# A hand-planned attention and gated-MLP kernel: the planner's rule for the shared SBUF port, and two kinds of work that may move from GpSimd to VectorE

## The chip, the cores and the metric

The kernel runs on one core of a Trainium2 chip. A core has five engines that run their own instruction streams: TensorE (PE in the profile; its weight loads are PEld), VectorE (DVE), ScalarE (ACT), GpSimd (POOL) and SyncE (SP), which only issues DMAs. They work on SBUF, the on-chip memory, and on PSUM, where TensorE leaves its sums. The metric is the device time of one execution in microseconds (us); less is better.

## The reference

There are eight batches of 576 positions with eight heads of 64. Each head's attention is the sum of two: one over q, k and v averaged in groups of four positions (144 of them), repeated fourfold, and one over the band of positions closer than four.

```python
q_d, k_d, v_d = (mean over groups of 4 positions)
out_up = np.repeat(sm_attn(q_d, k_d, v_d), 4, axis=2)
scores = np.where(abs(i - j) < 4, scale * q @ k.T, -1e9)
out_local = softmax(scores) @ v
x = (out_up + out_local), heads side by side: (8, 576, 512)

h = np.maximum(x @ w_in, 0)                 # 512 -> 1024
u, v = h[..., :512], h[..., 512:]
v_n = (v - mean(v)) / sqrt(var(v) + 1e-6)
v_s = w_spatial @ v_n + b_spatial           # over the 576 positions
out = (u * v_s) @ w_out
```

## The kernel before, in words

Two heads are worked on together, on 64 partitions each, so there are 32 **attentions**, n = 0 to 31, four to a batch. An attention has, in the kernel's own names: a load of q and k (`qk`) and of windows of v (`v`); `sum1` and `sum2`, which add q and k in groups of four (lines 523 and 526, on GpSimd) and `sum3`, which scales and spreads q's sums; `S`, the band's scores on TensorE (line 553), then `mask`, `max`, `sub`, `exp`, `sum`, `inv` and `norm`, a softmax; `T`, its transposes (line 606); `AV` (line 686), the product with v; and for the averaged part `Sd` (line 618), `maxd`, `expd`, `invd`, `normd`, `Td` (654) and `AVd` (672). `xf` adds both parts, and `xhi` and `xlo` (lines 703 and 705) split the sum in two numbers of TensorE's 32-bit format, since every large product is made of three such partial products. `load_down` brings the averaged v: one DMA by SyncE's queue (`tv0`, line 494) and three that add onto it in memory, by GpSimd's queue (`tv`, line 496); each of the four waits until the one before has landed.

A batch's gated MLP then has five blocks `V` (line 732; the fifth, of 64 positions, is line 737) for the half that is normalized, eight `U` (786), eight `SP` over the positions (lines 804 to 807), and five `O` (834, 839). A `V` block is followed by relu, statistics on VectorE, `rstd` on GpSimd (759), `apply` on VectorE (746), `vhi` on ScalarE (763) and `vlo` (765). These share four row buffers, and four PSUM banks (`pm`).

The weights of w_in and w_out come as 64-bit floating point. Twelve pieces (`piece64`) take them apart on VectorE with integer operations (`e1`, `m1`, `m2`, `e3`), on ScalarE (`e2`), multiply mantissa and power of two on GpSimd (`m3`, line 424), and split the result (`whi`, `wlo`). w_spatial comes as 32-bit and is only split. All weights are decoded while the first attentions run.

**The order** is not the program's. Every operation is handed to a `Plan` with its engine, a duration in ns, its buffers, whether it uses the SBUF port that VectorE and GpSimd share (`port=True`), and a rank. `Plan.run` then goes through a simulated time: for every engine it takes, of the operations that could start within `NEAR` ns of the first that could, the one of the lowest rank; among the engines' candidates it emits the earliest. That fixes the order of the instructions on each engine, which then run in that order and wait for one another by semaphores. The ranks of an attention's steps are its number n plus the entries of `RANK` (one for batch 0, one for batch 1, one for all later ones), and those of a batch's blocks come from `MRANK`. `ON` says, by a letter for each attention or block, which of several engines does an operation (a `Way`): D is VectorE, P is GpSimd, A is ScalarE; the last letter holds for all that follow. For `mask`, T lets TensorE add the mask by two more matmuls (line 546), so that VectorE doesn't add it. Before 110 us of planned time, planned idle of TensorE is filled with matmuls on constants (`warm`, line 872).

Of the kernel before, what the change touches and what calls it, by code (L numbers as in the profile page):

```python
# [15 lines left out]
ALU = mybir.AluOpType  # L16
# [60 lines left out]
class Plan:  # L77
# [54 lines left out]
    def run(self, near=150.0, stay=0.0, dma=(1500.0, 4.2, 500.0), emit=True):  # L132
# [3 lines left out]
        port = 0.0  # L136
# [4 lines left out]
        mode = "F"  # L141
# [7 lines left out]
        while left:  # L149
            best = None  # L150
            for eng, ops in todo.items():
                t0 = free[eng]
                first, found = None, []
                for o in ops:
                    t = o.ready if o.ready > t0 else t0
                    if o.port and port > t:
                        t = port
                    if o.mode:
                        t += TURN[mode + o.mode]
# [24 lines left out]
            t, o = best  # L184
# [52 lines left out]
RANK = {"load": [17.851, 23.264, -5.516],  # L237
        "tv": [12.974, 22.991, -23.395],
        "sum": [2.845, 5.024, -10.777],
        "S": [10.209, 18.391, 8.905],  # L240
        "E": [7.352, 3.618, -15.279],
        "N": [4.14, 4.621, -14.612],
        "T": [-15.681, 6.591, 2.05],
        "Sd": [-48.304, -1.568, 6.234],
        "Nd": [3.291, -4.748, 39.225],
        "Td": [-6.413, -29.413, 1.538],
        "AVd": [5.75, -12.653, -2.551],
        "AV": [-15.213, 2.555, -20.265],
        "X": [-1.494, 10.399, 1.329]}
MRANK = {"V": [[-0.574, 0.623], [2.224, 0.01], [-11.217, 0.975]],  # L250
        "U0": [[2.087, 0.31], [1.571, 0.675], [1.966, 0.126]],
        "S0": [[-14.652, 7.66], [4.784, 0.04], [8.452, 0.274]],
        "U1": [[5.341, 132112000.0], [-12.254, 4.82], [3.082, 3.0]],
        "O0": [[25.153, 0.02], [8.915, 8.0], [13.043, 2.786]],
        "S1": [[-8.328, 0.085], [-22.165, 0.04], [2.505, 0.191]],
        "O1": [[-2.911, 13597.0], [9.3, 0.531], [7.824, 0.451]]}
EVICT = 8.0
WRANK = {"WV": [2.481, 0.044],
        "WU": [3.142, 1.539],
        "WSP": [-1.507, 1.688],  # L260
        "WO": [-21.154, 0.035]}
NEAR = 109.733
STAY = 18.724
# [4 lines left out]
ON = {"mask": "TTDDD",  # L268
# [7 lines left out]
def tile_kernel(ctx, tc, qk, vw, v4, w_in, wT, bsp, w_out, out, emit=True):  # L276
    nc = tc.nc
# [640 lines left out]
```

## Time and profile before

| | |
|---|---|
| median of 3 runs | 639.61 us (637.89, 639.61, 641.01) |
| the profiled execution's own time | 635.72 us |
| its span, from the first to the last record | 633.8 us |
| mean granted clock of TensorE | 0.976 of full speed |
| busy: TensorE, VectorE, ScalarE, GpSimd | 592.8, 412.1, 307.3, 229.7 us |
| moved by DMA | 56.95 MB |

The profile is of one execution, whose time of 635.72 us is 1.9 us more than its span and lies 3.9 us under the median of the runs. A busy time of TensorE holds also the filling matmuls of the start. A wait is put down to the instruction that ended last before it, and the chain of waits goes back from the last instruction to what released each one. Section 2 of the page cuts the span in 40 slices of 15.8 us.

### The profile page before, as it was taken

The page shows a single profiled execution, that of the slowest core. Times are in us where ns is not written, and L with a number is a line of the kernel's source. Part 1 is how long each engine was busy: PE and PEld are TensorE (multiplying, and loading weights), DVE is VectorE, ACT ScalarE, POOL GpSimd, SP SyncE. Part 2 cuts the span into 40 slices and gives each one's busy share as a digit, 9 for nine tenths or more (in the row PEclk, how much of TensorE's full clock was granted, in tenths as well). Part 3 has the DMA queues.
Part 4 walks back from the last instruction along what each step waited for, and adds up shares of the span by engine and source line. Part 5 has one row for each costly group of instructions (what it writes and reads, how often), then busy time and mean ns, then how long its engine had stood idle before and what let it go on. Part 6 is the DMA issues. An engine that isn't in the chain of part 4 may idle for free.

```text
span 633.8 us, 14573 instructions
## 1 busy us (share of the span) xinstructions
PE 592.8 (94%) x5987; PEld 518.9 (82%) x5987; DVE 412.1 (65%) x887; ACT 307.3 (48%) x790; POOL 229.7 (36%) x220
## 2 busy tenths in 40 slices
PE   5737998999999999998999979999899999999997
PEld 2415777988998889887898878988798888998895
DVE  5898989989769566585647565485756756334230
ACT  3537766564544455544554354443655455424222
POOL 6574464514324352145413462044521452004100
PEclk9778898999999999999999979999999999999999
DMA  9982643544017123243404323054222201000102
GB/s 241 281 200 82 187 99 110 148 103 133 23 57 199 25 60 100 83 107 55 134 9 156 58 72 100 2 169 57 77 84 90 61 24 42 1 35 1 51 1 74
DMA packets 37382, 56.95 MB, mean 90 GB/s; under 512 B 3650, under 2 KB 24130, under 8 KB 37316
## 3 DMA queue, kind: packets, MB, share of 16 engines
q1 hardware_dynamic: 35012, 48.94, 25.4%
q0 software_dynamic: 2304, 7.08, 7.2%
q8 instruction: 47, 0.77, 0.5%
q14 instruction: 19, 0.16, 0.1%
HBM read 46.57 MB, written 9.44 MB: 88 GB/s over the span
## 4 chain that ended last, share of the span: by engine, by line
PE 75%; DVE 11%; POOL 4%; issue 4%; DMA 3%; ACT 3%; POOLq 0%; ACTq 0%; DVEq 0%
PE pmb L834 5%; PE pma L804 5%; PE pmc L786 5%; PE pma L834 5%; PE pmd L786 5%; PE pmb L804 4%; PE pmc L804 3%; PE pmd L804 3%; PE pma L786 3%; PE pmb L786 2%; PE pmd L834 2%; PE pmc L732 2%; PE pmc L834 2%; PE paa L686 2%; PE pma L732 2%
## 5 line engine op out<-in xcount | busy, mean ns | idle before, releaser
L804 PE MATMUL pma<-wsp,vha 128*128 128x320 f32 (+1 forms) x240 | 36.8, 302 | 0.0
L705 POOL TENSOR_TENSOR xa<-xfa,xa 128x576 fp32r<-128x576 f32 x6 | 11.2, 1865 | 70.3 <-ACT xa L703 70.3
L804 PEld LDWEIGHTS pma<-wsp,vha 128*128 128x128 f32 x240 | 33.6, 188 | 0.0
L834 PE MATMUL pmb<-wo,ga 128*128 128x512 f32 x132 | 33.0, 399 | 0.0
L804 PE MATMUL pmb<-wsp,vha 128*128 128x256 f32 (+1 forms) x192 | 30.2, 308 | 0.0
L834 PEld LDWEIGHTS pmb<-wo,ga 128*128 128x128 f32 x132 | 24.2, 188 | 5.1
L804 PEld LDWEIGHTS pmb<-wsp,vha 128*128 128x128 f32 x192 | 27.5, 196 | 0.9 <-issue 0.8
L526 POOL TENSOR_TENSOR kdb<-suma 128x288 f32<-128x288 f32 x16 | 14.5, 905 | 36.5 <-PE pmb L618 33.9
L834 PE MATMUL pma<-wo,ga 128*128 128x512 f32 x108 | 27.3, 402 | 0.0
L523 POOL TENSOR_TENSOR suma<-qka 128x576 f32<-128x576 f32 x17 | 20.9, 1231 | 17.1 <-DMA qka<-qk_dram 16.8
L804 PE MATMUL pmd<-wsp,vha 128*128 128x256 f32 (+1 forms) x168 | 25.1, 298 | 0.0
L523 POOL TENSOR_TENSOR suma<-qkb 128x576 f32<-128x576 f32 x15 | 18.0, 1203 | 17.8 <-DMA qkb<-qk_dram 17.2
L804 PE MATMUL pmc<-wsp,vha 128*128 128x256 f32 (+1 forms) x168 | 24.2, 293 | 0.0
L834 PEld LDWEIGHTS pma<-wo,ga 128*128 128x128 f32 x108 | 19.7, 188 | 5.2 <-issue 1.0
L804 PEld LDWEIGHTS pmd<-wsp,vha 128*128 128x128 f32 x168 | 23.1, 188 | 0.2 <-issue 0.2
L804 PEld LDWEIGHTS pmc<-wsp,vha 128*128 128x128 f32 x168 | 22.7, 188 | 0.1
L566 DVE TENSOR_TENSOR sa<-pab,mask 128x384 f32<-128x384 f32 (+1 forms) x28 | 12.4, 482 | 15.7 <-PE pab L553 15.7
L872 PE MATMUL pma<-mask_b,mask_a 128*128 128x512 bf16 x62 | 18.4, 437 | 3.2 <-DVE mask_a L325 3.2
L594 ACT ACTIVATE sa<-sa 128x640 f32<-128x640 f32 x17 | 12.5, 738 | 18.3 <-DVE sa L572 18.2
L496 POOL DMA_DIRECT2D tva<-v_dram x12 | 10.9, 909 | 23.5 <-DMA tva<-v_dram 23.1
L496 POOL DMA_DIRECT2D tvb<-v_dram x12 | 10.4, 866 | 24.4 <-DMA tvb<-v_dram 24.0
L705 POOL TENSOR_TENSOR xb<-xfa,xb 128x576 fp32r<-128x576 f32 x7 | 10.2, 1450 | 24.7 <-ACT xb L703 24.7
(568 smaller groups left out, 1838.8 us busy)
## 6 DMA issues: line engine op xcount, KB each, us to landing
qka<-qk_dram SPq DMA_DIRECT2D x17, 576.0 KB, 4.0
qkb<-qk_dram SPq DMA_DIRECT2D x15, 576.0 KB, 5.7
stg<-w_in_dram SPq DMA_DIRECT2D x8, 512.0 KB, 5.3
tva<-v_dram POOLq DMA_DIRECT2D x12, 288.0 KB, 5.7
tvb<-v_dram POOLq DMA_DIRECT2D x12, 288.0 KB, 4.5
out_dram<-rowc SPq DMA_DIRECT2D x9, 256.0 KB, 2.3
va<-vw_dram SPq DMA_DIRECT2D x11, 192.0 KB, 4.4
vb<-vw_dram SPq DMA_DIRECT2D x11, 192.0 KB, 3.2
```

The source lines that it names most:

```text
L496: plan.op("POOL", 850, lambda r=r: nc.gpsimd.dma_start(t.ap, v4[b, r], accum_op=ALU.add), w=[t], rank=rank + 2.0 + 0.3 * r, kb=288, name="tv")
L523: nc.gpsimd.tensor_tensor(sb.ap.rearrange("p x (g r) -> p x g r", r=2), x[:, :, :, :2], x[:, :, :, 2:], op=ALU.add)
L526: nc.gpsimd.tensor_tensor(kb.ap, sb.ap[:, :, ::2], sb.ap[:, :, 1::2], op=ALU.add)
L566: nc.vector.tensor_tensor(sv, pv, mask[:, None, None, :].broadcast_to(list(pv.shape)), op=ALU.add)
L594: plan.op("ACT", 643, lambda: nc.scalar.activation(s.ap, s.ap, AF.Exp, scale=1.0 / 8.0), w=[s], rank=R["E"], name="exp")
L686: nc.tensor.matmul(pv.ap[h * 64:h * 64 + 64, c:c + QB[w + 1] - QB[w]], vb.ap[k, w], pT.ap[k, blk, q0:q0 + QB[w + 1] - QB[w]], start=True, ...
L705: plan.op(xl, 0, lambda: side(xl).tensor_sub(x.ap[:, 1, :], xf.ap, f(x.ap[:, 0, :])), r=[xf, x.sub(0)], w=[x.sub(1)], rank=R["X"], name="xlo")
L732: nc.tensor.matmul(ps.ap, xs[c].ap[:, i, t * P:(t + 1) * P], win[:, c, j, FF:], start=(c == 0 and (i, j) == (0, 0)), stop=(c == NC - 1 and ...
L786: nc.tensor.matmul(ps.ap[:, :n], win[:, c, i, ft * P:(ft + 1) * P], xs[c].ap[:, j, HA[h]:HA[h + 1]], start=(c == 0 and (i, j) == (0, 0)), ...
L804: nc.tensor.matmul(ps.ap[:, :n], vh.ap[:, c, i, fs], wsp[:, c, j, hs], start=(c == 0 and (i, j) == (0, 0)), stop=False)
L834: nc.tensor.matmul(ps.ap, g.ap[:, c, o1:o1 + P], wo[:, c, j, :], start=(c == 0 and (i, j) == (0, 0)), stop=(c == NF - 1 and i == 1))
L872: nc.tensor.matmul(ap.rearrange("p (j k) -> p j k", k=64), mask_a, mask_b[:, None, :].broadcast_to([P, 8, 64]), start=True, stop=True)
```

## The change

Three things change. In `Plan.run` the engines' candidates are now compared by the time at which they ask to start: when their inputs, buffers and engine are free. Before, they were compared by the time at which they could start, with the wait for the port and TensorE's change of tile shape in it. So the port goes to the one that asks first. `sum1` and `sum2` of an attention, and `m3` of a weight piece, become a `Way` and may run on VectorE. And all tables of ranks and of engines are new numbers, which reorders the program on every engine.

```diff
@@ Plan.run
-                    if o.port and port > t:
-                        t = port
-                    if o.mode:
-                        t += TURN[mode + o.mode]
 ...
                     if ok:
-                        found.append((t, o.rank - stay if o.mode == mode else o.rank, o))
+                        ask = t
+                        if o.port and port > t:
+                            t = port
+                        if o.mode:
+                            t += TURN[mode + o.mode]
+                        found.append((t, o.rank - stay if o.mode == mode else o.rank, ask, o))
 ...
-                t, _, o = min((x for x in found if x[0] <= first + near), key=lambda x: (x[1], x[0]))
-                if best is None or t < best[0]:
-                    best = (t, o)
+                t, _, ask, o = min((x for x in found if x[0] <= first + near), key=lambda x: (x[1], x[0]))
+                if best is None or ask < best[0]:
+                    best = (ask, t, o)
 ...
-RANK = {"load": [17.851, 23.264, -5.516],
-        "tv": [12.974, 22.991, -23.395],
+RANK = {"load": [-6.425, 5.791, -0.091],
+        "tv": [-13.62, 1.562, -8.346],
 ...
-ON = {"mask": "TTDDD",
-        "norm": "PDDDDDPDD",
-        "xlo": "DDDDDPDPP",
-        "normd": "ADDAPAAAD",
-        "vlo": "DPPDPDDDDPP"}
+ON = {"sum": "DDPPDDDPD",
+        "m3": "DDPPPPDDDDDD",
+        "mask": "TTTTTTTTD",
+        "norm": "PDDDDPDDD",
+        "xlo": "PDPDPDDPP",
+        "normd": "APAAAAADP",
+        "vlo": "PDPPPPPPPPP"}
 ...
         def m3():
-            nc.gpsimd.tensor_tensor(mb.ap, mb.ap, eb.ap, op=ALU.mult)
+            if pr.eng == "POOL":
+                nc.gpsimd.tensor_tensor(mb.ap, mb.ap, eb.ap, op=ALU.mult)
+            else:
+                nc.vector.scalar_tensor_tensor(mb.ap, mb.ap, 2.0**-20, eb.ap, op0=ALU.mult, op1=ALU.mult)
 ...
-        plan.op("POOL", 1251, m3, r=[eb], w=[mb], rank=rank, port=True, name="m3")
-        return split(dst_hi, dst_lo, lambda: mb.ap, 2.0**-20, [mb], rank, FF, key)
+        pr = Way("m3", {"WV": 0, "WU": NC, "WO": 2 * NC}[key[0]] + key[1], P=("POOL", 1251, True), D=("DVE", 602, True))
+        plan.op(pr, 0, m3, r=[eb], w=[mb], rank=rank, name="m3")
+        return split(dst_hi, dst_lo, lambda: mb.ap, 2.0**-20 if pr.eng == "POOL" else 1.0, [mb], rank, FF, key)
 ...
-        plan.op("POOL", 1150, sum1, r=[qkb], w=[sb], rank=R["sum"], port=True, name="sum1")
-        plan.op("POOL", 660, sum2, r=[sb], w=[kb], rank=R["sum"], port=True, name="sum2")
+        s1 = Way("sum", n, P=("POOL", 1150, True), D=("DVE", 669, True))
+        s2 = Way("sum", n, P=("POOL", 665, True), D=("DVE", 370, True))
+        plan.op(s1, 0, sum1, r=[qkb], w=[sb], rank=R["sum"], name="sum1")
+        plan.op(s2, 0, sum2, r=[sb], w=[kb], rank=R["sum"], name="sum2")
```

By the tables, VectorE takes over 29 of the 32 pairs of sums and 8 of the 12 `m3`; GpSimd takes `normd` of all attentions from 8 on (VectorE had them) and every `vlo` but one; TensorE adds the mask for 8 attentions (before 2). In numbers of instructions VectorE has 58 sums, 8 `m3`, 12 mask additions fewer (two for each of 6 attentions), 25 `normd` fewer and 5 `vlo` fewer. The changed kernel's lines lie 4 to 10 below those of before: line 523 becomes 531, 705 becomes 715, 496 becomes 504.

Three places show what moved. The first is VectorE ahead of the first `V` block, where the fourth attention's `xd` (its `xlo`, the last input of that block) is made. Before it is VectorE's 114th instruction, and the masks and maxima of attentions 4 and 5 and a piece of w_spatial stand ahead of it:

```order
L598 TENSOR_TENSOR sa<-sa,sma 128x640
L566 TENSOR_TENSOR sb<-paa,mask 128x2x3x64
L566 TENSOR_TENSOR sb<-paa,mask 128x2x2x64
L696 TENSOR_TENSOR xfa<-pab,dnb 128x2x116 x2
L698 TENSOR_TENSOR xfa<-pab,dnb 128x112
L569 TENSOR_REDUCE mxb<-sb 128x10
L378 SCALAR_TENSOR_TENSOR wsp<-stg,wsp 128x576
L631 TENSOR_SCALAR smdb<-smdb 96x3
L632 RECIPROCAL smdb<-smdb 96x3
L572 TENSOR_TENSOR sb<-sb,mxb 128x640
L705 TENSOR_TENSOR xd<-xfa,xd 128x576
```

Now it is the 100th, and among what stands ahead is an `m3` (line 431):

```order
L594 TENSOR_REDUCE sma<-sa 128x10
L382 SCALAR_TENSOR_TENSOR win<-rowd,win 128x512
L416 SCALAR_TENSOR_TENSOR rowa<-stg,rowa 128x512
L706 TENSOR_TENSOR xfa<-paa,dnb 128x2x116 x2
L708 TENSOR_TENSOR xfa<-paa,dnb 128x112
L431 SCALAR_TENSOR_TENSOR rowb<-rowb,rowa 128x512
L406 TENSOR_SCALAR rowc<-stg 128x512
L715 TENSOR_TENSOR xd<-xfa,xd 128x576
```

The second is GpSimd where a batch's `V` blocks begin, in batches 3 to 5 (numbered from 0). Before, the three adding DMAs of `tv` stand after both of the batch's last `xlo`, the third of them behind the first `rstd` (line 759) and ahead of the first `vlo` (765):

```order
L705 TENSOR_TENSOR xb<-xfa,xb 128x576
L523 TENSOR_TENSOR suma<-qka 128x576
L496 DMA tva<-v_dram 72x1024
L526 TENSOR_TENSOR kdb<-suma 128x288
L496 DMA tva<-v_dram 72x1024
L759 TENSOR_TENSOR stc<-stc,mhalf 128x1
L496 DMA tva<-v_dram 72x1024
L765 TENSOR_TENSOR vha<-rowb,vha 128x512
L759 TENSOR_TENSOR sta<-sta,mhalf 128x1
```

Now the first of them stands ahead of the last `xlo`, and the other two follow each other ahead of the first `rstd`:

```order
L715 TENSOR_TENSOR xa<-xfa,xa 128x576
L504 DMA tva<-v_dram 72x1024
L651 TENSOR_TENSOR eda<-eda,smda 96x432
L715 TENSOR_TENSOR xb<-xfa,xb 128x576
L504 DMA tva<-v_dram 72x1024 x2
L769 TENSOR_TENSOR stc<-stc,mhalf 128x1
L775 TENSOR_TENSOR vha<-rowc,vha 128x512
L769 TENSOR_TENSOR sta<-sta,mhalf 128x1
```

The third is VectorE at the end of such a batch, where a `sum1` now stands in its queue (line 531; it reads the q and k of the attention after next, whose load can start when the scores of the attention just masked are done), ahead of the next `maxd` and `xf`:

```order
L576 TENSOR_TENSOR sb<-pab,mask 128x2x3x64
L576 TENSOR_TENSOR sb<-pab,mask 128x2x2x64
L579 TENSOR_REDUCE mxb<-sb 128x10
L582 TENSOR_TENSOR sb<-sb,mxb 128x640
L594 TENSOR_REDUCE smb<-sb 128x10
L531 TENSOR_TENSOR suma<-qkb 128x576
L632 TENSOR_REDUCE mxda<-pma 96x3
L706 TENSOR_TENSOR xfa<-paa,dnb 128x2x116 x2
L708 TENSOR_TENSOR xfa<-paa,dnb 128x112
```

TensorE's order at these places: before, the blocks of a later batch begin V V V V U `V(64 positions)` T U AV S AVd U U Td T; now V V U V V U T `V(64 positions)` U U U Sd AV S AVd T Td. Up to the second batch's first `V` block TensorE has done one `S`, `Sd`, `T`, `Td`, `AV`, two `AVd` and one `O` fewer than before; the other blocks done by then are the same.

More of the change, by code (lines that the diff above doesn't have):

```diff
@@ L178, in run @@
                     continue
[L179 to L181 removed]
+                t, _, ask, o = min((x for x in found if x[0] <= first + near), key=lambda x: (x[1], x[0]))
+                if best is None or ask < best[0]:
+                    best = (ask, t, o)
             if best is None:
                 raise RuntimeError("no piece can start: " + str(sorted({(o.name, o.rank) for ops in todo.values() for o in ops})[:40]))
[L184 removed]
+            _, t, o = best
             if o.mode:
@@ L231, in run @@
         return end
-RANK = {"load": [17.851, 23.264, -5.516],
-        "tv": [12.974, 22.991, -23.395],
[L239 to L249, printed above, removed]
@@ L262 @@
-NEAR = 109.733
-STAY = 18.724
-WARM = 110000.0
-ON = {"mask": "TTDDD",
-        "norm": "PDDDDDPDD",
-        "xlo": "DDDDDPDPP",
-        "normd": "ADDAPAAAD",
-        "vlo": "DPPDPDDDDPP"}
+RANK = {"load": [-6.425, 5.791, -0.091],
+        "tv": [-13.62, 1.562, -8.346],
+        "sum": [7.232, 2.664, -2.313],
+        "S": [-5.456, -8.108, -3.65],
+        "E": [-2.935, 8.439, 4.083],
+        "N": [-20.365, 3.051, 3.136],
+        "T": [3.06, 5.617, -6.295],
+        "Sd": [-18.648, -4.028, 1.939],
+        "Nd": [-2.732, 2.402, -1.457],
+        "Td": [7.722, -5.93, 1.317],
+        "AVd": [-13.128, 1.0, 1.083],
+        "AV": [-1.585, -10.971, -1.682],
+        "X": [-1.109, -4.0, 4.59]}
@@ new lines @@
+MRANK = {"V": [[-6.123, 0.551], [-1.086, 0.028], [-14.993, 3.036]],
+        "U0": [[3.982, 0.015], [1.649, 0.423], [-9.629, 4.068]],
+        "S0": [[1.127, 0.03], [0.23, 3.042], [3.342, 0.027]],
+        "U1": [[2.468, 0.21], [-7.158, 41.047], [1.939, 0.01]],
+        "O0": [[10.423, 0.043], [-3.057, 3.396], [-1.764, 19.425]],
+        "S1": [[2.091, 1386.76], [-9.258, 0.282], [-2.998, 0.191]],
+        "O1": [[-13.345, 1489.49], [6.908, 3186040.0], [7.786, 1.714]]}
+EVICT = 8.0
+WRANK = {"WV": [-8.825, 0.01],
+        "WU": [3.09, 0.206],
+        "WSP": [-1.275, 0.06],
+        "WO": [-16.539, 7.189]}
@@ L275, in tile_kernel @@
+NEAR = 120.124
+STAY = 7.582
+WARM = 110000.0
+ON = {"sum": "DDPPDDDPD",
[5 more added lines that the diff above has]
+        "vlo": "PDPPPPPPPPP"}
 @with_exitstack
@@ L522, in sum1 @@
             x = qkb.ap.rearrange("p x (g r) -> p x g r", r=4)
-            nc.gpsimd.tensor_tensor(sb.ap.rearrange("p x (g r) -> p x g r", r=2), x[:, :, :, :2], x[:, :, :, 2:], op=ALU.add)
+            side(s1).tensor_tensor(sb.ap.rearrange("p x (g r) -> p x g r", r=2), x[:, :, :, :2], x[:, :, :, 2:], op=ALU.add)
         def sum2():
-            nc.gpsimd.tensor_tensor(kb.ap, sb.ap[:, :, ::2], sb.ap[:, :, 1::2], op=ALU.add)
+            side(s2).tensor_tensor(kb.ap, sb.ap[:, :, ::2], sb.ap[:, :, 1::2], op=ALU.add)
         def sum3(h):
```

11 lines of the change are left out of this document (removed).

## The prediction

> **What bounds the kernel now.** I read the page's first two sections, then TensorE's waits, then stretches of the span engine by engine.
>
> ```profile
> PE 592.8 (94%) x5987; PEld 518.9 (82%) x5987; DVE 412.1 (65%) x887; ACT 307.3 (48%) x790; POOL 229.7 (36%) x220
> PE   5737998999999999998999979999899999999997
> PEclk9778898999999999999999979999999999999999
> ```
>
> TensorE is busy for nearly all of the span behind the seventh slice (110 us). Ahead of it, it is idle or filled, and at slices 19, 24 and 29 there are dents, at the second of them in the clock as well. TensorE's waits after 100 us are three rows:
>
> ```profile
> PE pab L686 <- ACT probTa L608: 6.6, 3, 3.3
> PE paa L606 <- DVE sb L598: 1.6, 1, 1.6
> PE pmd L732 <- DVE ud L815: 0.7, 1, 0.7
> ```
>
> So everywhere else TensorE's own work sets the time, and a faster VectorE or GpSimd gains nothing there. The first row is three waits at the begin of batches 3 to 5. The chain of waits shows where the first comes from:
>
> ```profile
> 271.49 0.65 PE pmc L672 x8
> ...
> 279.02 4.42 DMA tvb<-v_dram
> ...
> 283.98 0.83 POOL tvb L496
> ...
> 285.40 3.21 issue
> ...
> 288.62 0.42 POOL tvb L496
> ...
> 296.61 0.70 ACT probTa L608
> ...
> 297.35 0.85 PE pab L686 x38
> 298.20 0.05 PE paa L553
> ...
> 298.26 0.59 PE paa L553 x35
> 298.85 0.65 PE pma L672 x8
> ```
>
> GpSimd stands 3.2 us at 285.4 until an adding DMA of `tv` has landed. Everything behind it (each `vlo`, then the next `rstd`) is late by that, ScalarE's queue stands behind a `vhi`, and the copy of the probabilities that `AV` needs comes at 296.6. The longest of the three waits, 3.3 us, has a second price:
>
> ```profile
> 372.00:375.00 3.00, 3.00 (x30) 2.52 (x23) 2.42 (x9) 1.01 (x4) 1.77 (x2) 0.51 0.36 93
> 375.00:378.00 3.00, 3.00 (x16) 3.00 (x16) 1.55 (x3) 2.06 (x5) 2.49 (x2) 0.50 0.77 217
> ```
>
> After it the granted clock is 0.51 and 0.50 for 6 us, so 6.0 x 0.495 = 3.0 us of work are lost. The other two waits (1.7 and 1.6 us: what is left of 6.6) show no such stretch in the page's row.
>
> The start is another regime. The columns below are the stretch, its length, then busy time of TensorE, its weight loads, VectorE, ScalarE, GpSimd, and last the clock and the DMA:
>
> ```profile
> 30.52:74.20 43.68, 28.32 (x444) 19.95 (x445) 41.08 (x79) 24.12 (x71) 23.44 (x18) 0.84 0.53 147
> 74.20:103.10 28.90, 25.48 (x175) 21.73 (x168) 25.85 (x54) 21.04 (x55) 16.73 (x17) 0.99 0.54 137
> 103.10:142.26 39.16, 39.16 (x467) 36.21 (x469) 36.15 (x73) 22.93 (x63) 15.45 (x13) 0.97 0.46 119
> ```
>
> From 30.5 to 142.3 us VectorE is busy 103.1 of 111.7 us, 92%: it sets the pace of the head, in which all weights are decoded, until the second batch's inputs are made. TensorE is full only from 103 on.
>
> **The change, part by part.** Three terms.
>
> *First, the head.* What VectorE has to do between the masks of attention 2 (at 30.52) and the `xf` of attention 7 (at 142.26), the last attention of batch 1, decides how early batch 1's first `V` block may start. Prices are by the groups of instructions and single rows of VectorE and GpSimd:
>
> ```profile
> L705 DVE TENSOR_TENSOR xa<-xfa,xa 128x576 fp32r<-128x576 f32 x2 | 1.5, 746 | 0.0
> L412 DVE SCALAR_TENSOR_TENSOR rowc<-stg,rowc 128x512 int32<-128x512 int32 x5 | 3.4, 683 | 0.0
> L641 DVE TENSOR_TENSOR edb<-edb,smdb 96x432 f32<-96x432 f32 x13 | 7.8, 599 | 0.1
> L566 DVE TENSOR_TENSOR sa<-pab,mask 128x384 f32<-128x384 f32 x14 | 7.7, 551 | 15.7 <-PE pab L553 15.7
> L523 POOL TENSOR_TENSOR suma<-qka 128x576 f32<-128x576 f32 x17 | 20.9, 1231 | 17.1 <-DMA qka<-qk_dram 16.8
> L526 POOL TENSOR_TENSOR kda<-suma 128x288 f32<-128x288 f32 x16 | 15.1, 943 | 8.9 <-PE pmd L618 4.2 <-DMA qka<-qk_dram 2.1 <-PE pmc L618 2.1
> L424 POOL TENSOR_TENSOR rowd<-rowd,rowc 128x512 f32<-128x512 f32 x3 | 5.4, 1809 | 3.7 <-DVE rowc L412 3.7
> 7.77 1.50 DVE L417 TENSOR_SCALAR rowd<-stg 128x512 int32<-128x512 int32 x1
> 7.67 1.31 POOL L424 TENSOR_TENSOR rowb<-rowb,rowa 128x512 f32<-128x512 f32 x1 [3.83 <-DVE rowa L412]
> ```
>
> Rows that follow one another on VectorE overlap by 0.07 us, so I count 0.07 less than a row: 0.67 for a `sum1` (nearest row: `xlo`, as wide; its ends are 0.67 and GpSimd's 1.23), 0.37 for a `sum2` (half as wide; up to 0.94), 0.61 for an `m3` (as L412; up to 1.81). In this stretch the change adds 11 sums (5.9 us) and 6 `m3` (3.6), 2 decoding steps (1.3) and one more maximum and `sub` (0.7 + 0.7, taken together as 1.1). It takes away 10 mask additions at 0.4 (4.0), 2 `normd` (1.1), 2 `xlo` (1.3), one `vlo` (0.6), one `norm` (0.7), one `maxd` (0.5), 2 small steps of `inv` and 2 of `invd` (0.5), two gates and six `glo` (2.9; these move behind). The sum of all rows in the stretch is 89.1 us in the order of before and 89.3 us in the new one: **no work is gained**. What can shrink is the rest of the 111.7 us. VectorE was busy 103.1, so 14.0 us lie in its rows over the 89.1, and 8.7 us it was idle. The 14.0 are rows like the one at 7.77, 1.50 us long beside a GpSimd row of 1.31 that began at 7.67, where the same shape takes 0.42 elsewhere. I put them down to GpSimd's wide instructions in the stretch: 32 before (8 `m3`, 18 sums, 6 others), so 0.44 us each. The new order has 21 there, 9.2 us. With the idle time kept at 8.7, the `xf` of attention 7 comes 89.3 + 9.2 + 8.7 = 107.2 us after the scores of attention 2, so at 30.3 + 107.2 = 137.5.
>
> ```profile
> 29.00 1.35 PE L553 MATMUL paa<-qka 64*64 64x64 f32 x40 [0.35 <-ACT probTb L608]
> 149.70 0.85 PE L732 MATMUL pmc<-win,xe 128*128 128x512 f32 x3
> L705 POOL TENSOR_TENSOR xa<-xfa,xa 128x576 fp32r<-128x576 f32 x6 | 11.2, 1865 | 70.3 <-ACT xa L703 70.3
> 233.42 2.79 PE pmd L834 x12
> 278.50 0.25 PE pmc L654 x3
> 11.28 0.43 PE L546 MATMUL pab<-mask_b,mask_a 128*128 128x320 bf16 x2
> ```
>
> The scores of attention 2 end at 30.3; they still stand behind the transposes of attention 1, so I leave them there. Behind `xf` come `xhi` (0.7), `xlo` on GpSimd (1.9) and 0.3 for semaphores, and the block may begin three quarters of its 2.8 us earlier, since this input is read last: 137.5 + 2.9 - 2.1 = 138.3, against 149.7 before. But by then TensorE has done less: an `O` (2.8), an `S`, an `AV` and an `AVd` (0.6 + 0.85 + 0.65 and 0.15 for the change of shape), another `AVd` (0.65), a `Td` (2 x 0.25), and `Sd` and `T`, some 0.6 each: 7.4 us. So the head gains 149.7 - 138.3 - 7.4 = **4.0 us**. Its ends: with no slowed rows at all it is 129.1, a gain of 13.2; with the 14.0 kept and the idle time doubled it is 150.9 + 0.8, a loss of 9.4. The six additional pairs of mask matmuls (0.43 us each) fall into the head's idle of TensorE.
>
> *Second, the begins of batches 3 to 5.* The waits there cost 6.6 + 3.0 = 9.6 us. In the new order the second and third DMA stand back to back ahead of the first `rstd`; so the question is when the third is issued. From the end of the last `AVd` that reads the buffer to the first adding DMA before: 272.1 to 279.0, 6.9 us. That `AVd` now ends 12.1 us ahead of the `V` block (`T`, `Td`, `O`, `Sd`, a group `AV` `S` `AVd`, `O`, `Td`, `O` of 64: 0.6 + 0.5 + 2.8 + 0.65 + 2.3 + 2.8 + 0.5 + 1.9). The three then go out at -5.2, -0.2 (5.0 later, as 279.02 to 283.98) and +4.7 (4.6 and 5.0 between the rows), and the first `rstd` can start at 5.5, where its statistics are ready at 2.8 + 1.8 = 4.6. It is late by 1 us, not by 3 to 4. And what was hurt is no longer near: the `AV` stands some 7 us behind the `T` (the block of 64, three `U` and an `Sd`), where before one `U` was between them. So I take all 9.6 us as gone; the other end is none.
>
> *Third, new waits.* In the steady batches VectorE gets 4 x (0.67 + 0.37) and loses 4 x 0.53 of `normd`, +2.0 us a batch, and has room for it:
>
> ```profile
> 281.00:353.00 72.00, 70.32 (x743) 63.02 (x742) 46.23 (x103) 35.40 (x93) 27.63 (x25) 1.00 0.32 85
> POOL suma L523 <- DMA qkb<-qk_dram: 17.2, 7, 3.5
> POOL suma L523 <- DMA qka<-qk_dram: 16.8, 8, 4.4
> L641 POOL TENSOR_TENSOR eda<-eda,smda 96x432 f32<-96x432 f32 x1 | 2.2, 2157 | 1.3 <-ACT qdb L530 1.3
> ```
>
> 46.2 of 72 us are used. `normd` on GpSimd (one row, 2.16 us; 0.9 if like its narrower `sum2`) lengthens the way from `Sd` to `Td`, but a `Td` reads the `Sd` before the last, so some 10 us cover it; without that cover it would be 1.6 us for each of 24. The three rows of waits above held 2.3 us besides the `AV`; new places of that kind I count at 2.0, with ends of 0 and 10. Together: 635.7 - 4.0 - 9.6 + 2.0 = 624.1 us for an execution like the profiled one, and with the 3.9 us by which the median stands over it **628 us**.
>
> The third rows' waits of `sum1` for its load are 34.0 us in 15 waits. They now fall on VectorE.
>
> Two rules of the Trainium skill bear on this. "SBUF — State Buffer", section "Who interferes with whom", says that a VectorE instruction with two SBUF inputs and a GpSimd instruction that reads SBUF block each other, the first to issue holding the port to its end. The pair at 7.67 and 7.77 agrees in that the later one is the long one. By that rule the sums on VectorE, with two SBUF inputs, would now hold up GpSimd's `normd` and be held up by it, which speaks against the steady half of the change. "TensorE: Matmul & The Clock Gate", section "What's actually happening", has the clock halved after an idle window of about 3.4 us; here a wait of 3.3 us was enough.
>
> **The rivals.** (a) *The head gains nothing*, since VectorE stands idle longer where it no longer has masks to do: 628 + 4 = 632. For it speaks the sum of 89.3 against 89.1; against it that 11 wide GpSimd instructions leave the stretch. (b) *The waits at the batch begins stay*, because DMAs that follow each other hold GpSimd at the one place where `rstd` waits: 628 + 9.6 = 637.6. Against it speaks the earlier `AVd`; for it that the three take 9.6 us from the first to the third. (c) *The head loses*, at its upper end: 628 + 13.4 = 641.4. The port rule would push here: two-input sums meeting what GpSimd keeps. (d) *Slower: the load of q and k now holds VectorE's queue.* Behind `sum1` stand `maxd` and the `xf` of the batch's last attention. The `xf` has 3.0 us of cover (6.8 us from `AV` to the `V` block less 3.8 for `xf`, `xhi`, `xlo`) and 2.1 more, as above. It decides once a load lands some 5 us after VectorE gets to its `sum1`; the mean wait was 34.0/15 = 2.3, the longest 4.4, on an engine that got there at other times. If six batches then wait as long as the mean of the three waits above (2.2 us) and half of them lose the clock's 3.0, that is 6 x 2.2 + 9 = 22 us: 650. (e) That the order isn't what the tables say can't be: the instructions stand as the front part shows.
>
> **How the numbers follow.** The forecast, 628, has 0.58, with a range of its own of 620 to 635; (a) 0.12, (b) 0.10, (c) 0.07, (d) 0.13. Runs of this kernel differ by 0.5%, 3.2 us, so "faster" is under 636.4 and "slower" over 642.8. Faster takes the forecast and (a): 0.70. The same takes (b) and (c): 0.17. Slower is (d): 0.13. The range holds all but (d) and a better head than its lower end: 619 to 641.
>
> **What would show it.** Right: no wait of an `AV` for the copy of the probabilities at the begins of batches 3 to 5, and a clock of 1.0 throughout them; batch 1's first `V` block at 136 to 141 us; VectorE's wait for loads under 30 us, with none of TensorE's behind it. Wrong: a `V` block of a later batch waiting for `xlo`, waits of TensorE over 5 us in sum after 140 us, or a first `V` block of batch 1 later than 143 us, where the head would no longer gain.

## The result, and the profile after

The changed kernel takes 614.74 us (four executions, 612.55 to 617.94), the kernel before, measured beside it, 640.31 us (four, 637.89 to 644.25). The ratio is 0.960, 95% interval 0.953 to 0.966: 25.6 us faster. The forecast was 628 us with a range of 619 to 641; the direction was right and the gain more than twice the 12 us forecast. The profiled execution is the slowest of the four (617.94 us, span 616.0). Executions of one kernel scatter with the granted clock, and where some of them lie over 1.5% above the fastest, a difference is given without these as well.

The first two sections of its page, to be read against the two rows of before:

```profile
PE 590.8 (96%) x5987; PEld 518.0 (84%) x5987; DVE 400.7 (65%) x915; ACT 309.5 (50%) x793; POOL 183.0 (30%) x185
PE   6688888999999999999999999999999999999997
PEclk9889979999999999999999999999999999999999
```

The three dents of TensorE behind slice 18 are gone, and GpSimd has 46.7 us less to do. TensorE's waits after 100 us are one row:

```profile
PE pma L664 <- ACT edb L649: 1.8, 1, 1.8
```

The copy of the probabilities is no longer waited for. The stretch of the second begin, first before, then after (columns as in the prediction):

```profile
330.00:390.00 60.00, 56.69 (x618) 49.61 (x618) 36.62 (x82) 26.13 (x64) 24.33 (x22) 0.94 0.34 87
```

```profile
330.00:390.00 60.00, 60.00 (x605) 54.17 (x604) 41.41 (x96) 29.87 (x78) 19.18 (x19) 1.00 0.31 83
```

TensorE is busy throughout, at full clock. And the head: batch 1's first `V` block, at 149.70 before, now starts here.

```profile
134.95 0.87 PE L742 MATMUL pmd<-win,xe 128*128 128x512 f32 x3
```

Up to that row the profiled execution gained 149.70 - 134.95 = 14.75 us, of which 7.4 are TensorE work that is only done later: 7.35. (Counted in the traces, TensorE is busy 477.1 us behind that row in the changed kernel and 470.0 in the kernel of before with its three waits removed, below: 7.1.) Behind that row the kernel before has 633.8 - 149.70 = 484.1 us, the changed kernel 616.0 - 134.95 = 481.05 with 7.4 us of work more: 10.45. Together 17.8 us, the difference of the two profiled spans. The remaining 7.8 of the 25.6 us lie in which executions were profiled: that of before was 4.6 us under the median of the four measured beside the changed kernel, that of after 3.2 over its own.

The next rows are the stretch from the start to that `V` block, before and after; the third busy time is VectorE's, the fifth GpSimd's:

```profile
0.00:149.70 149.70, 119.91 (x1430) 95.33 (x1431) 130.68 (x259) 86.47 (x231) 75.83 (x78) 0.92 0.60 161
```

```profile
0.00:134.95 134.95, 113.65 (x1305) 90.06 (x1306) 115.39 (x254) 83.58 (x221) 45.52 (x55) 0.92 0.61 171
```

VectorE does nearly the same number of instructions there, 259 and 254, in 15.3 us less. Why can be read from single rows. First three of VectorE's in the kernel before, then GpSimd's beside them:

```profile
42.92 1.23 DVE L631 TENSOR_SCALAR smda<-smda 96x3 f32<-96x3 f32 x1
...
44.27 1.10 DVE L587 TENSOR_SCALAR sma<-sma 128x10 f32<-128x10 f32 x1
...
45.54 1.37 DVE L641 TENSOR_TENSOR eda<-eda,smda 96x432 f32<-96x432 f32 x1
```

```profile
41.53 2.59 POOL L424 TENSOR_TENSOR rowc<-rowc,rowa 128x512 f32<-128x512 f32 x1 [2.26 <-DVE rowa L412]
44.09 1.25 POOL L424 TENSOR_TENSOR rowd<-rowd,rowb 128x512 f32<-128x512 f32 x1
45.31 1.14 POOL L523 TENSOR_TENSOR suma<-qka 128x576 f32<-128x576 f32 x1
```

A row over 96x3 numbers, 0.15 us elsewhere, lasts until 44.15, when GpSimd's row ends (44.12). The next does the same, 45.37 against 45.34; the third ends 0.46 behind GpSimd's third (46.91 against 46.45), about its own 0.53. GpSimd's first row, beside VectorE's decoding, lasted 2.59 us where the next of its kind took 1.25. Now two rows of VectorE of the changed kernel that read PSUM, and GpSimd's beside them:

```profile
42.12 0.81 DVE L585 TENSOR_REDUCE mxa<-paa 128x10 f32<-128x640 f32 x1
42.97 0.89 DVE L591 TENSOR_TENSOR sa<-paa,mxa 128x384 f32<-128x384 f32 x2
```

```profile
41.78 1.68 POOL L715 TENSOR_TENSOR xa<-xfa,xa 128x576 fp32r<-128x576 f32 x1 [0.33 <-ACT xa L713]
```

They keep their length. I worked this out for all rows of VectorE that start ahead of that `V` block: "own" is the sum of what each row lasts undisturbed (the lower quartile of its form, that is of its operation, shapes and number of inputs, PSUM or not, over 17 traces), "stretched" what the rows last beyond it. Rows overlap by some 0.07 us, so that own and stretched add up to more than the busy time. The last column is GpSimd's own rows of 200 columns or more. All values are us of one profiled execution each; the kernels that are new here come below.

| kernel | `V` block at | VectorE busy | own | stretched | wide GpSimd rows |
|---|---|---|---|---|---|
| before | 149.7 | 130.7 | 127.7 | 20.2 | 61.7 |
| after | 135.0 | 115.4 | 127.2 | 3.7 | 33.2 |
| head of before | 148.9 | 131.5 | 127.7 | 21.0 | 61.5 |
| the same, masks on TensorE | 148.9 | 128.4 | 122.9 | 22.5 | 61.1 |
| head of after | 131.7 | 115.5 | 127.1 | 4.0 | 33.2 |
| the same, 12 more VectorE rows | 144.8 | 127.7 | 135.2 | 9.0 | 33.8 |
| the same, masks on VectorE | 138.1 | 123.8 | 131.9 | 8.1 | 34.2 |
| the same, 24 more GpSimd rows | 146.7 | 131.8 | 127.1 | 20.5 | 62.9 |
| the same, sums and `m3` on GpSimd | 137.1 | 111.0 | 111.5 | 12.4 | 62.1 |
| after, old rule of the planner | 153.9 | 132.4 | 135.2 | 14.3 | 36.3 |

From before to after VectorE has the same work of its own, 16.5 us less stretch and 15.3 us less busy time, and the block comes 14.75 us earlier.

### The profile page after: what moved, and what is told of

Read it like the earlier page. It is cut to its first block, busy times and chain, and to the rows that moved or that the text cites. A ratio compares the mean times of both kernels' runs of the same rounds, so it can differ in the third digit from the quotient of the medians.

```text
span 616.0 us, 14561 instructions
## 1 busy us (share of the span) xinstructions
PE 590.8 (96%) x5987; PEld 518.0 (84%) x5987; DVE 400.7 (65%) x915; ACT 309.5 (50%) x793; POOL 183.0 (30%) x185
## 4 chain that ended last, share of the span: by engine, by line
PE 85%; DVE 7%; ACT 3%; DMA 2%; issue 1%; POOL 1%; SPq 0%; ACTq 0%; POOLq 0%
PE pmc L844 6%; PE pmb L814 5%; PE pmb L796 4%; PE pmd L796 4%; PE pmd L814 4%; PE pma L814 4%; PE pma L844 4%; PE pmd L742 4%; PE pma L742 4%; PE pmc L814 3%; PE pmc L796 3%; PE pma L796 3%; PE pmb L844 3%; PE pmb L742 3%; PE pmc L742 3%; PE pmd L844 2%
## 5 line engine op out<-in xcount | busy, mean ns | idle before, releaser
L844 PE MATMUL pmc<-wo,ga 128*128 128x512 f32 x132 | 33.0, 399 | 0.0
L814 PE MATMUL pmb<-wsp,vha 128*128 128x320 f32 (+1 forms) x204 | 30.8, 299 | 0.0
L814 PE MATMUL pma<-wsp,vha 128*128 128x256 f32 (+1 forms) x204 | 30.4, 297 | 0.0
L844 PEld LDWEIGHTS pmc<-wo,ga 128*128 128x128 f32 x132 | 24.3, 188 | 5.9 <-issue 0.6
L651 POOL TENSOR_TENSOR edb<-edb,smdb 96x432 f32<-96x432 f32 x13 | 16.9, 1298 | 28.7 <-DVE smdb L642 23.6
L651 POOL TENSOR_TENSOR eda<-eda,smda 96x432 f32<-96x432 f32 x12 | 13.9, 1158 | 31.5 <-DVE smda L642 16.7
L844 PE MATMUL pma<-wo,ga 128*128 128x512 f32 x84 | 21.1, 400 | 0.0
L504 POOL DMA_DIRECT2D tva<-v_dram x12 | 10.6, 884 | 33.0 <-DMA tva<-v_dram 23.1
L715 POOL TENSOR_TENSOR xa<-xfa,xa 128x576 fp32r<-128x576 f32 x7 | 10.2, 1460 | 33.4 <-ACT xa L713 33.4
L882 PE MATMUL pma<-mask_b,mask_a 128*128 128x512 bf16 x51 | 16.5, 457 | 3.2 <-DVE mask_a L329 3.2
L844 PEld LDWEIGHTS pma<-wo,ga 128*128 128x128 f32 x84 | 15.3, 188 | 3.5 <-issue 0.4
L582 DVE TENSOR_TENSOR sa<-sa,mxa 128x640 f32<-128x640 f32 x12 | 17.4, 1452 | 0.3
L594 DVE TENSOR_REDUCE smb<-sb 128x10 f32<-128x640 f32 x16 | 13.0, 814 | 4.5 <-ACT sb L604 4.2
L775 POOL TENSOR_TENSOR vha<-rowd,vha 128x512 fp32r<-128x512 f32 x9 | 12.1, 1348 | 12.2 <-ACT vha L773 12.2
```

The source lines that it names most:

```text
L504: plan.op("POOL", 850, lambda r=r: nc.gpsimd.dma_start(t.ap, v4[b, r], accum_op=ALU.add), w=[t], rank=rank + 2.0 + 0.3 * r, kb=288, name="tv")
L582: nc.vector.tensor_tensor(s.ap, s.ap, mx.ap[:, :, None].broadcast_to([P, NW, 64]), op=ALU.subtract)
L594: nc.vector.tensor_reduce(sm.ap, s.ap, axis=AX.X, op=ALU.add)
L651: side(nd).tensor_tensor(ed.ap, ed.ap, smd.ap[:96, :, None].broadcast_to([96, 3, G]), op=ALU.mult)
L715: plan.op(xl, 0, lambda: side(xl).tensor_sub(x.ap[:, 1, :], xf.ap, f(x.ap[:, 0, :])), r=[xf, x.sub(0)], w=[x.sub(1)], rank=R["X"], name="xlo")
L775: plan.op(vl, 0, lambda: side(vl).tensor_sub(vh.ap[:, t, 1, :], vr.ap, f(vh.ap[:, t, 0, :])), r=[vr, vh.sub(t, 0)], w=[vh.sub(t, 1)], rank ...
```

## Experiments on the kernel before

**How much do its executions differ?** The kernel before, unchanged.

> The kernel before, unchanged, so that span and granted clock of several of its executions are known. Theory 1 (the profiled execution was a lucky one): its other executions have spans of 637 to 642 us and a granted clock below the profiled 0.976, by about the difference in time (0.7%, so about 0.970); the cause would be stretches of half clock after waits that the profiled execution had only once. Theory 2 (the offset is something outside the span, so the same for every kernel): the spans stay near 633.8 and only the time around them differs.

Ten executions: 637.01 us median, 635.09 to 642.27; 25 of the kernel before in the same session 638.13 (634.16 to 644.67). The spans lie from 632.2 at a granted clock of 0.981 to 640.2 at 0.964 (two more, 642.0 and 642.6, at 0.964 and 0.956). Theory 1 holds in part: it is the spans that scatter, and they follow the clock, but the profiled execution, at 633.8, stood only 1.8 us under the median span of the 35 (635.6), and nine of them are shorter.

**The second term alone.** The DMAs of `tv` for batches 5 to 7 are held back in the plan until the last `U` block of the batch two before (`u_of`). TensorE's and VectorE's lines keep their order by this; in GpSimd's queue the DMAs change place, and around them an `xlo` and a pair of sums.

```diff
-        plan.op("SP", ..., v4[b, 0]), w=[t], rank=rank, ...)
+        plan.op("SP", ..., v4[b, 0]), w=[t], after=[u_of[b - 2]] if b >= 5 else (), rank=rank, ...)
```

> The kernel before with one thing moved: the four DMAs of tv for batches 5 to 7 are planned behind the last U block of the batch two before, so they no longer stand among the first V blocks of batches 3 to 5. Theory (second term of the prediction): the three waits of an AV for the copy of the probabilities go and with them the half clock after one of them, 9.6 us of an execution like the profiled one (634 to 624 in span), about 630 in the median. If runs with more half clock make up the median's distance to the profiled execution, up to 14 us. Rival: something else in those places is late (rstd, the vhi on ScalarE), then the waits only change their name and the gain is under 3 us.

630.35 us (627.88 to 631.41), 7.8 less than 638.13; ratio 0.988, 0.983 to 0.993. TensorE's waits after 100 us:

```profile
PE paa L606 <- DVE sb L598: 1.6, 1, 1.6
PE pmd L786 <- DVE rowc L755: 0.5, 1, 0.5
PE pmd L732 <- DVE ud L815: 0.2, 1, 0.2
PE pmc L732 <- DVE ub L815: 0.2, 1, 0.2
PE pmc L732 <- DVE ua L815: 0.2, 1, 0.2
```

The three waits are gone, and nothing of their size stands in their place. In this profile 474.5 us lie behind batch 1's first `V` block, in those of before 484.1 and 482.0. So the place of the adding DMAs is worth 7.5 to 9.6 us by the profiles and 7.8 by the medians, and the 9.6 of the prediction lie within the interval.

**VectorE's masks.** The first eight masks are added on TensorE, in the order of before.

```diff
-        pe_mask = sc.pick == "T"
+        pe_mask = n < 8
```

> The kernel before, in its own order, but the masks of attentions 2 to 7 are added on TensorE. VectorE loses 12 additions of 0.40 us and its six subtractions read PSUM (0.88 a pair in place of 0.735), 4.0 us less work in the head. Theory (VectorE sets the head's pace): batch 1's first V block comes 4 us earlier, at about 145.7, and the time falls by 4 (to about 636). If the subtractions that read SBUF were among the rows that GpSimd stretches, up to 5.5. Rival (another engine or the loads set the pace): V block within 1 us of 149.7 and no change in time.

638.06 us against 638.13, ratio 1.001 (0.997 to 1.005): no change. The 4 us forecast for it are outside the interval.

**The sums alone.** As the changed kernel has them, in the order of before.

```diff
-            nc.gpsimd.tensor_tensor(sb.ap...
+            (nc.gpsimd if n in (2, 3, 7) else nc.vector).tensor_tensor(sb.ap...
```

(and the same for `sum2`)

> The kernel before, in its own order, with sum1 and sum2 of all attentions but 2, 3 and 7 executed by VectorE. Theory of the prediction (each wide GpSimd row costs VectorE 0.44 us by contention, a pair of sums on VectorE costs it 1.04): in the head's stretch about 6 pairs move, plus 6.2 us of work and minus 5.3 of contention, so the head changes by under 2 us; batches 3 to 5 keep their waits unless the first adding DMA comes earlier. Time 636 to 642. Rival 1 (the sums on VectorE are by themselves what gains): a gain of 8 us or more. Rival 2 (sum1's wait for its load holds VectorE's queue): slower by over 5 us.

637.76 us, ratio 1.000 (0.996 to 1.003). The sums do not gain by themselves, and as `sum1` in VectorE's queue they do not lose either. In its profile 29 GpSimd rows of 200 columns or more stand ahead of batch 1's first `V` block, where before has 46, and VectorE's rows are stretched by 19.1 us, before by 20.2: fewer wide GpSimd rows alone hardly lessen the stretch.

## Experiments on the head

Since the executions differ by 8 us, the head was then run by itself: the same plan, but nothing is issued behind batch 1's first `V` block. All later work and its outputs are left out.

```diff
             if emit:
-                o.fn()
+                o.fn(); emit = o.name != "V1"
```

> The head alone: the kernel before, in its own order, but nothing is issued after the first V block of batch 1, so the time is that of the head (all blocks of batches 1 to 7 behind this one, and the outputs that they would write, are left out). In the profiled execution that block ends at 149.7 + 2.8 = 152.5; two other profiled executions of the same head had it at 151.7 and 154.9. Theory A (the profiled head was a lucky one): the median span is 154 to 156. Theory B (it was typical): 152 to 153.

> The same cut of the changed kernel: its first V block of batch 1 ends at 134.95 + 2.8 = 137.7 in the profiled execution, the slowest of four whose spans were 616.0, 613.1, 612.5 and 610.6. Theory A (its other executions differ in the head): median span 133 to 136, so that after the 7.4 us of work not yet done the head gains 11 to 15 us, not the 4.0 of the prediction. Theory B: 137 to 138, and the head gains 7 to 8.

Before 159.54 us (156.46 to 160.24), after 140.67 us (139.53 to 143.10). These kernels end 3.0 and 3.2 us behind the block (154.7 against 148.90 + 2.8 in the profile of the first, 137.7 against 131.67 + 2.8 in that of the second), which the expectations left out. With that the median spans, 157.8 and 138.9, put the block's start at 152.0 and 132.9, where the profiled executions had 149.70 and 134.95: theory A for both. For before that rests on three of its five executions (159.54, 160.21 and 160.24); by the other two its block starts at 149.9, which is theory B. The difference of the medians is 18.9 us; without those three and the longest of after (143.10) it is 17.6. Less the 7.4 of work not yet done the head gains 10.2 to 11.5, more than twice the forecast.

> The head of before with the masks of attentions 2 to 7 added on TensorE, order unchanged: 12 VectorE additions of 0.40 us less, six subtractions now from PSUM (4.0 us less of VectorE's work; TensorE has 2.6 us more). VectorE sets the pace: 4 us less than the head of before, up to 5.5 if the subtractions were stretched. Another pace: less than 1 us. The whole kernel with this edit showed no change in time, so either the head does not gain or it is given back later.

158.26 us (157.14 to 158.93), where VectorE lost 4 us of work: inside the scatter of the head of before, whose two shorter executions are 156.46 and 158.43. In both profiles the `V` block starts at 148.9. The table shows where the work went: own falls by 4.8, but the busy time only by 3.1, since stretched rises by 1.5 (rows with two inputs from SBUF rise from 8.4 to 11.9, TENSOR_SCALAR rows, which have one tensor and scalars, fall from 12.4 to 10.4). The rest became idle time: VectorE's waits for TensorE, which now adds the masks, rise from 3.5 to 7.9 us, and those for GpSimd fall from 5.3 to 3.4.

Then work was added to the head of after: first twelve VectorE rows.

```diff
+                o.name in ("m2",) and self.more()
+    plan.more = lambda: nc.vector.tensor_tensor(junk, one, one, op=ALU.add)
```

> The head of after with 12 more VectorE additions (128x512, from SBUF to a buffer nobody reads, one behind each m2 of the weights' decoding, 0.6 to 0.7 us each, 8 us in all), nothing else changed. VectorE sets the pace of the new head too: 6 to 8 us longer. If VectorE has slack there (17.5 us idle of 128 in the profiled execution): under 3 us.

152.66 us (152.12 to 156.30): 12.0 longer for 8 us of work (12.6 without the longest of each). VectorE does set the pace of the new head. The table holds the rest of the price: with 8.1 us more of its own, VectorE's rows are stretched by 5.0 us more, and its busy time rises by 12.2. TensorE's clock fell too; the stretch from 40 to 60 us without and with the twelve rows:

```profile
40.00:60.00 20.00, 17.91 (x249) 12.14 (x246) 19.26 (x45) 14.52 (x38) 7.60 (x6) 1.00 0.67 170
```

```profile
40.00:60.00 20.00, 19.63 (x246) 13.78 (x248) 17.66 (x39) 13.73 (x36) 6.78 (x6) 0.59 0.39 103
```

That the lower clock adds to the time is not shown: VectorE's busy time accounts for the 12 us without it.

Next the masks of attentions 2 to 7 back on VectorE (`pe_mask = n < 2`).

> The head of after (140.7 us), order unchanged, with the masks of attentions 2 to 7 added on VectorE again (12 rows of 0.40 us, and six subtractions from SBUF in place of a pair from PSUM: plus 4.0 us of VectorE's work). The same edit the other way round changed the head of before by 1.3 us. Theory V: 4 to 6 us longer. Theory P (VectorE can do it beside GpSimd's rows, since they read PSUM): under 2.5 us longer.

148.71 us (145.61 to 150.17), 8.0 longer. Three of the four had a clock of 0.883 to 0.885; the profiled one, at 0.929, is 145.61, 5.8 longer than the three shorter executions of the head of after (139.82 median), and its `V` block starts 6.4 us later. So theory V fits within the scatter, and theory P, under 2.5, is out: own rises by 4.8 (4.0 are the edit, the rest rows that now come ahead of the later block), stretched by 4.1.

Now GpSimd rows, 24 of them, and no work for VectorE.

```diff
+                o.name in ("m2", "e3") and self.more()
+    plan.more = lambda: nc.gpsimd.tensor_tensor(junk, one, one, op=ALU.add)
```

> The head of after (140.7 us) with 24 more GpSimd additions (128x512, from SBUF to a buffer nobody reads, one behind each m2 and each e3 of the weights' decoding), some 1.25 us each, 30 in all; VectorE's work is unchanged. Theory V: under 2 us longer. Theory C: 24 x 0.44 = 10.6 longer. Theory P: 15 to 30 longer, less where VectorE reads PSUM beside them. In VectorE's rows the stretch should be on those that read SBUF alone (TENSOR_SCALAR and two-input rows) and not on those that read PSUM.

153.41 us (151.53 to 154.45): 12.7 longer, 0.53 us for each row (12.3 without the two of 154.17, the profiled one, and 154.45); VectorE's own work is the same, its stretch grows by 16.5. Theory V is out, and theory C comes near. By kind of VectorE's rows that lie beside a GpSimd row: 17 TENSOR_SCALAR rows from SBUF are 7.1 us longer in sum, 31 rows with two inputs from SBUF 12.7, 39 rows with an input from PSUM 0.2, six reductions from SBUF nothing. It is so in every trace: over 17 of them each of the 483 VectorE rows that last over 0.3 us beyond their own lies beside a GpSimd row, while of 2781 rows with two inputs, one from PSUM, none lasts over 0.03 us longer, and of 770 reciprocals from SBUF none over 0.01.

The Trainium skill says in "SBUF — State Buffer", section "Who interferes with whom": a VectorE instruction with at most one SBUF input, outside the fast modes, does not contend with GpSimd, and reductions never do. The rows with two inputs, the reductions and the reciprocals agree. The TENSOR_SCALAR rows have one tensor from SBUF and are stretched all the same; the section has `tensor_scalar` among the operations that can enter a fast mode and then contend, and no row here names its mode (in the decoding 128x512 lasts 0.41 us, against 0.68 with two inputs as wide).

Last, what the change moved to VectorE was given back to GpSimd, in the new order: 9 `sum1`, 8 `sum2`, 8 `m3`.

```diff
-            side(s1).tensor_tensor(sb.ap...
+            nc.gpsimd.tensor_tensor(sb.ap...
-            if pr.eng == "POOL":
+            if True:
```

> The head of after (140.7 us), order unchanged, with the 9 sum1, 8 sum2 and 8 m3 that it has on VectorE given back to GpSimd. VectorE's own work falls by 9 x 0.67 + 8 x 0.37 + 8 x 0.61 = 13.9 us. Theory V (VectorE's own work is the pace; 8 us more of it made the head 12 longer): 14 to 20 us shorter, 121 to 127. Theory C (the prediction's price, 0.44 us of contention for each of 25 more wide GpSimd rows = 11): 3 shorter, 136 to 139. Theory P (GpSimd's wide rows and VectorE's rows that read only SBUF pass one at a time, so a move to GpSimd costs the difference of the two durations, 9 x 0.5 + 8 x 0.6 + 8 x 0.65 = 14.5): 150 to 157, and stretched rows of VectorE back.

144.93 us (143.97 to 145.34): 4.3 longer (5.1 against the three shorter executions of the head of after), though VectorE has some 15 us less of its own. None of the three numbers fits: stretched rises by 8.4, and VectorE is idle for 26.0 us ahead of the block, where it was 16.2. Of its waits 5.0 us are for ScalarE's `whi`, which in turn waits 17.0 us for GpSimd's `m3`. So the sums and `m3` on VectorE gain 4 to 5 us in this order.

## Experiments on the whole changed kernel

**The planner's rule.** All tables as changed, the comparison as before.

```diff
-                if best is None or ask < best[0]:
-                    best = (ask, t, o)
+                if best is None or t < best[0]:
+                    best = (t, t, o)
```

> The whole changed kernel with all its tables, but the planner compares the engines' candidates by the time they can start, as before; the order comes out anew on every engine. If the rule is what keeps GpSimd's and VectorE's SBUF rows apart: VectorE's rows of the head are stretched by over 10 us in sum again (2.3 with the rule, 19.9 before) and the time is 622 to 632. If the engines and ranks in the tables do it: stretched by under 5 us, and 612 to 620, unless the boundaries get new waits of TensorE, which the profile would show.

633.54 us (630.64 to 636.16), ratio to before 0.995 (0.991 to 0.999). Batch 1's first `V` block starts here:

```profile
153.90 0.94 PE L742 MATMUL pmc<-win,xe 128*128 128x512 f32 x3
```

19 us later than with the rule, and 477.0 us lie behind it (481.05 with the rule, so 4 of the 19 us come back there). With the same engine for every operation and about as much wide GpSimd work (26 rows ahead of the block, 25 with the rule), VectorE's rows are stretched by 14.3 us in place of 3.7, and 8.0 us more of VectorE's work stands ahead of the block. So the number of wide GpSimd rows doesn't decide; what they meet does, and the order sets that. The run reorders every engine, so it does not separate the stretch from what else the order changes. Nor does it show that the rule would gain with other tables; with those of before it was not run.

**Sums in the steady batches.** Those of attentions 8 to 31 back on GpSimd, order unchanged, beside the changed kernel once more.

> The changed kernel, order unchanged, with sum1 and sum2 of attentions 8 to 31 given back to GpSimd (24 pairs of the 29); in the steady batches VectorE has 4.2 us a batch less and GpSimd some 8 more. Theory (behind the head only the place of the adding DMAs mattered, and neither engine sets the time there): within 3 us of the changed kernel. If moving the sums off GpSimd is what keeps rstd, vlo and xlo in time: TensorE's waits at the batch begins come back, 5 to 12 us slower.

> The changed kernel once more, on the chip and beside the runs of the next two. It had 612.55 to 617.94 in four executions, with spans that follow the granted clock (0.983 with 616.0, 0.991 with 610.6). Theory: median 613 to 616; a second profile has batch 1's first V block within 3 us of 134.95 and what comes behind it within 2 us of 481.0, so that the scatter that is left lies in the head's clock. If the scatter lies behind the head, the second number differs by more.

616.95 us (614.67 to 619.71) and 615.42 (614.91 to 615.50, and one of 718.58 at a clock of 0.752, which was the profiled one; its trace is not used). In the first's profile 612.7 - 131.66 = 481.04 us lie behind the `V` block, in the changed kernel's 481.05. Behind the head the sums' engine is worth nothing. Whether the scatter that is left lies in the head was not settled by the second profile; but two executions of the same head differ by 3.3 us in the `V` block, 134.95 in the whole kernel and 131.67 in the head by itself.

**Two waits that were left.** `normd` of attention 4 on VectorE, right behind its `invd`, that of 5 on GpSimd; `invd` of 4 goes ahead of the first step of the bias piece.

```diff
-            if nd.eng == "ACT":
+            if nd.eng == "ACT" and n not in (4, 5):
...
-                side(nd).tensor_tensor(ed.ap, ...
+                (nc.gpsimd if n == 5 else nc.vector if n == 4 else side(nd)).tensor_tensor(ed.ap, ...
```

> The changed kernel with the two longest waits of TensorE behind 60 us attacked (2.55 us at 79.9 and 1.80 at 106.3, both Td behind a normd on ScalarE that stands in its queue behind work on loads and weights): the normd of attention 4 is done by VectorE right behind its invd, which goes ahead of the first step of the bias piece (lb); the normd of attention 5 is done by GpSimd, which is idle there for 13 us. TensorE's order is unchanged. Theory (these waits and the lower clock after them, 0.84 and 0.91 in the two stretches of 20 us behind, are lost time): 4 to 9 us faster than the changed kernel, 606 to 611. Rival (VectorE sets the pace there and the next wait takes their place): within 2 us.

615.88 us against 615.42: nothing. (Of the six executions one took 1139.62 us, and it was the profiled one; why is not known.) The same kernel again:

> The same kernel as the run before with the two normd moved (615.9 us, no faster than the changed kernel), for a profile that can be read. If the two waits at 79.9 and 106.3 are still there, the edit did not do what it should. If they are gone and other waits of TensorE of together 3 to 4.5 us stand in the 40 us behind, another engine sets the pace there and the waits only showed it. If they are gone and nothing stands in their place, the time must be lost by the clock.

616.31 us (615.83 and 616.80). TensorE's two longest waits after 60 us, first of the changed kernel, then with the edit:

```profile
PE pmd L664 <- ACT eda L649: 2.6, 1, 2.6
PE pma L664 <- ACT edb L649: 1.8, 1, 1.8
```

```profile
PE pma L664 <- POOL edb L651: 3.2, 1, 3.2
PE pma L664 <- ACT ub L799: 1.1, 1, 1.1
```

The first shrank, the second grew: TensorE got to `Td` earlier, and `normd` waited for an `invd` that stood behind the decoding of w_out in VectorE's queue. So in a last run `invd` and `normd` of both attentions follow right behind their `expd`.

> The changed kernel with invd and normd of attentions 4 and 5 issued right behind their expd: the invd of attention 5 no longer stands behind three pieces of w_out's decoding on VectorE (its exp was done at 96.2, its invd began at 105.4, and Td, which TensorE had got to at 104.5, waited 1.8 us; in the run before, where TensorE got there earlier, it waited 3.2 us for the same thing). The normd of 4 is VectorE's, that of 5 GpSimd's. If the order in VectorE's queue is what was late: no wait of a Td over 1 us behind 75 us, and 3 to 5 us faster than the changed kernel (610 to 612). If the w_out pieces themselves are the next limit (they are delayed by 0.5 to 1 us): the wait moves to the O block, and under 2 us is gained.

615.35 us (613.77 to 618.40): still nothing. No `Td` waits for `normd` any more, and others wait:

```profile
PE pma L882 <- DVE ud L825: 1.6, 1, 1.6
PE pma L628 <- ACT qdb L538: 1.4, 1, 1.4
PE pmc L796 <- DVE rowb L765: 1.4, 1, 1.4
PE pma L664 <- ACT ub L799: 1.0, 1, 1.0
```

Two are VectorE's own. Where VectorE sets the pace, TensorE's waits only say where it ran out of input.

## Why the prediction was right and wrong

- **The head, 4.0 us forecast, 10 to 11.5 measured, is the step that failed.** "No work is gained" was right: own is 127.7 and 127.2. What failed is the sentence behind it, "so 0.44 us each. The new order has 21 there, 9.2 us". The average price is sound (0.53 when 24 rows are put in blindly), but it isn't a price of the GpSimd row: it is paid only where VectorE's row beside it is a TENSOR_SCALAR or has two inputs, all from SBUF. In the new order 3.7 us are left in the whole head, and the `V` block came at 134.95, not 138.3. Two causes are shown: masks on TensorE, whose undoing adds 4.1 us of stretch and makes the head 5.8 to 8.0 longer for 4.0 us of work, and the new order, which without the rule has 14.3 stretched. In the old order the masks on TensorE gained nothing, so it takes both. I had quoted the rule of the Trainium skill (the section named above) only as speaking against the change; the half of it that names what does not contend was left out of the sum. The pair at 7.67 and 7.77, which I gave as a case of two SBUF inputs, isn't one: that VectorE row is a TENSOR_SCALAR.
- **Work added to VectorE in the new head cost half as much again** (12.0 for 8), since it brings new collisions: VectorE's busy time rose by 12.2. No term of the sum held that.
- **The 3.9 us by which the median stands over the profiled execution** were carried over to the new kernel, as if they were the program's. They were one execution's place in a scatter that follows the clock (1.8 us in the larger sample); the changed kernel's profiled execution stood 3.2 us on the other side. The heads alone show it: 10.2 to 11.5 us in the medians, 7.35 between the two profiled executions, of which one had its `V` block up to 2.3 us early and the other 2.0 to 2.9 late.
- **The boundaries, 9.6 us, were right** in size and in cause: 7.8 by the DMAs' place alone, the waits gone and the clock at 1.00.
- **New waits, +2.0, did not come.** After 110 us no row of TensorE's waits is left. Rival (d), the load that holds VectorE's queue, has this row of VectorE's waits and one of 0.7 us for the other buffer, where I allowed 30 us:

```profile
DVE suma L531 <- DMA qkb<-qk_dram: 7.8, 8, 1.9
```

- Rivals (a), (b) and (c) are out by the head's gain and the empty waits.
- **What is not settled:** 10.2 to 11.5 and 7.8 us make 18 to 19.3 of the 23 to 26 us measured. The rest is inside the uncertainty of the two, and no run separates it.

## What to carry to other kernels

Price a collision between VectorE and GpSimd by the pair: list which of VectorE's rows stand beside GpSimd's, and count only those that were stretched here, TENSOR_SCALAR and two-input rows that read SBUF alone. Taking work off VectorE need not gain: the masks given to TensorE gained nothing in the old order, where VectorE then waited for TensorE, and 5.8 us or more in the new. An order in which the wrong rows don't meet had 10.6 us less stretch, with the same engine for every operation. When a profiled execution lies off the median, ask in which part, before its offset is carried over.

## What was not expected of the hardware

- A VectorE row over 96x3 numbers took 1.23 us beside a GpSimd row (0.15 alone): a small row is not spared. A reciprocal over as few numbers never was stretched.
- The collision goes both ways: GpSimd's product of 1.25 us took 2.59 beside VectorE's decoding.
- The granted clock between 40 and 60 us fell from 1.00 to 0.59 when twelve rows were added to VectorE, not to TensorE, and the executions of one kernel spread over 8 us of span (632.2 to 640.2) with the clock (0.981 to 0.964).
